# Reordering the forward step of a segment-recurrent attention kernel: K and Q before V, V's second half behind the scores, V rows moved by three engines

## The chip, the cores and the metric

The kernel runs on one core of a Trainium2 chip. A core has engines with a queue of instructions each, which wait for one another through semaphores: TensorE (PE; the loads of its weights are shown apart, as PEld), VectorE (DVE), ScalarE (ACT), GpSimd (POOL) and SyncE (SP), whose queue only issues transfers. PE writes to PSUM, from where DVE and ACT copy ("evict") to SBUF. The metric is the device time of one execution in microseconds, as the median of several runs; lower is better.

## The reference

The program computes a block with a recurrent-memory attention and a SwiGLU feed-forward part, and all gradients. The forward attention is a chain: 2048 tokens are cut into 64 segments of 32, and each segment sees 8 memory rows that the segment before produced.

```python
for s in range(n_seg):                                   # 64
    xs = x[:, s*seg_len:(s+1)*seg_len, :]                # 32 tokens of 448
    h = jnp.concatenate([mem, xs], axis=1)               # 40 rows
    q = jnp.einsum('btd,dhe->bhte', h, Wq)               # 16 heads of 256
    k = jnp.einsum('btd,dhe->bhte', h, Wk)
    v = jnp.einsum('btd,dhe->bhte', h, Wv)
    scores = jnp.einsum('bhqe,bhke->bhqk', q, k) * scale
    scores = jnp.where(mask[None, None], scores, -1000000000.0)
    p = _softmax(scores, axis=-1)
    o = jnp.einsum('bhqk,bhke->bhqe', p, v)
    o = jnp.einsum('bhte,hed->btd', o, Wo)
    mem = o[:, :M, :]                                    # the next segment's memory
    outs.append(o[:, M:, :])
...
h = x + attention(layernorm(x)); out = h + (silu(n @ w_gate) * (n @ w_up)) @ w_down     # n = layernorm(h)
return (out, *gradients of x, mem0, Wq, Wk, Wv, Wo, w_gate, w_up, w_down)
```

## The kernel before

The program has four stages: the forward chain over 64 segments, the feed-forward part with its gradients, the backward chain over the segments, and a tail for weight gradients. The order of instructions on every engine is the order in which the program names them. The change touches only the forward chain, in `forward_chain`, and the helper `spin`.

A segment's 40 rows are treated as two kinds. Of a segment's 32 token columns in `hA`, 8 are the memory (written by the reduction at L518 at the end of the segment before) and 24 are tokens; the last 8 tokens of four segments are gathered in `hB` and projected a tile (four segments) ahead. That work on `hB`, and the Wo product of a tile's `oB` columns, are the "side work": `cur["u1"]`, `cur["u2"]` and `cur["u3"]` are its products (16, 8 and 8 of 512 columns, or 32, 16 and 16 of 224), `cur["e1"]` and `cur["e3"]` its evictions. In the last three segments there is none.

One segment runs thus. The names are those of the code:

- `proj` (L468): one half of K, Q or V, 16 products in four groups of 32 PE columns; the result (128 rows of 512) is evicted to `Kev`, `Qev` or `Vev` by DVE (`V`) or ACT (`A`). In the order: K0, K1, V0, Q0, Q1, and V1 in two pieces.
- `tr_half` (L474): four turnings of 128x128 of `Kev` or `Qev` against the identity; the copies out of PSUM make `kT` and `qT`, whose memory columns POOL fills from the side work (L693, L694).
- `v_shift`: the halves of `Vev` are 32 rows of a group of heads; eight copies of 32x512 put them side by side in `V_sb`, which has one buffer. Six of them are on DVE (`V`, L431), two on POOL (L731). Four row transfers (L646, `v_b_rows`, in SP's queue) add the rows that come from `hB`.
- `scores` (L505) in two halves, into `s_ps`, which holds the mask already (`mask_mm`, L488).
- softmax for each half: maximum (L738), subtraction (L740), exponential on ACT (L742), sum (L745), reciprocal (L747), multiply (L748) into `P_sb`.
- `u1`, `u2`, then `spin` (L847): products of the identity with itself into `s_ps`, which nobody reads before the mask overwrites it; two before the first turning of P (`p_turn`, L761) and one behind it. Then the mask for the next segment, the second turning, `u3`.
- copies of the turned P to `PT` (DVE and ACT), then two `v_shift` copies on DVE, then the product of P and V ("PV", L792) in four groups, evicted to `oA` by DVE and ACT in turns, then the Wo product (L583), the turning of its sum (L513) and the reduction to the next memory (L518).
- stores for the backward part: `KtokA`, `QtokA`, `Vtok` (SP's queue), `P_all` (POOL's queue). In the last segment `ff.load_first` issues six weight loads in POOL's queue.

PSUM has six rotating buffers for all of these (`ps1`) besides the two of the scores.

Of the kernel before, what the change touches and what calls it, by code (L numbers as in the profile page):

```python
# [15 lines left out]
P = 128  # L16
# [390 lines left out]
def forward_chain(k: _K, hA, NWIN, Wq_sb, Wk_sb, Wv_sb, Wo_sb, maskr, work, stage, ff):  # L407
    nc, tc = k.nc, k.tc
    S, D, M, H, Dh, HD = k.S, k.D, k.M, k.H, k.Dh, k.HD
    SEG, L, NSEG, NT, KC, DP, MC, DC = k.SEG, k.L, k.NSEG, k.NT, k.KC, k.DP, k.MC, k.DC  # L410
    X2 = k.aps["A_x"][0]
    ident, identf, dr = k.ident, k.identf, k.dr
# [3 lines left out]
    GF = HD // G  # L416
    NJ = GF // P
    HB = 512
# [6 lines left out]
    def ps1(dtype=FP32):  # L425
        if dtype == FP32:
            return k.pspool.tile([P, 512], FP32, tag="ps", name="psf")
        return k.pspool.tile([P, 1024], BF16, tag="ps", name="psh")

    def V(out, in_):  # L430
        nc.vector.tensor_copy(out=out, in_=in_)  # L431

    def A(out, in_):
        nc.scalar.copy(out=out, in_=in_)

    def slot(s):
        return s % NWIN

# [25 lines left out]
    def proj(ps, W_sb, stat, half, kcs=range(4)):  # L464
        for kc in kcs:
            for g in range(G):
                c0 = g * GF + half * HB
                nc.tensor.matmul(ps[32 * g:32 * g + 32, :], lhsT=stat(kc), rhs=W_sb[0:DB, kc, c0:c0 + HB],  # L468
                                 start=(kc == 0), stop=(kc == KC - 1))

    def tr_half(ev, half):
        pt = ps1(BF16)
        for j in range(4):
            nc.tensor.transpose(pt[:, j * P:(j + 1) * P], ev[:, half * HB + j * P:half * HB + (j + 1) * P], ident[:, :])  # L474
        return pt[:, 0:HB].rearrange("p (j g t) -> p j g t", j=4, g=G)

    def fm_view(dst, half, t0, t1):
        return dst[:].rearrange("p (g j) n -> p j g n", g=G)[:, 4 * half:4 * half + 4, :, t0:t1]
# [4 lines left out]
    S_ps = k.s_ps  # L483
    S_v = [x[0:NR, 0:HQ * L].rearrange("p (h n) -> p h n", n=L) for x in S_ps]

    def mask_mm(half):
        for gg in range(2):
            nc.tensor.matmul(S_ps[half][QB * gg:QB * gg + L, 0:HQ * L], lhsT=ident[0:L, 0:L], rhs=maskr[:, 0:HQ * L],  # L488
                             start=True, stop=False, skip_group_check=True)
# [4 lines left out]
    def hsel(x, half):  # L494
        return x[0:NR].rearrange("p (a b i) n -> p a b i n", a=2, b=2)[:, :, half, :, :]

    def hview(x):
        return x.rearrange("p (a i) n -> p a i n", a=2)
# [87 lines left out]
    def o_units(t):  # L586
        T = tiles[t]
        st = {}

        def mm(i0, i1):  # L590
            for i in range(i0, i1):
                for c in range(4 * i, 4 * i + 4):
                    wo_mm(st["pO"], T.oB[:, c, :], c, c % 2, c < 2, c >= MC - 2)

        def u1():
            st["pO"] = ps1(FP32)
            mm(0, 4)

        def e1():
            pass  # L600

        def u2():
            mm(4, 6)

        def u3():
            mm(6, 8)

        def e3():
            A(partB[:, 0:2 * DB], st["pO"][:, 0:2 * DB])

        def ut():
            st["y"] = turn(partB)

        def et():
            for kc in range(KC):
                gsum(T.aT[0:DB, kc, :].rearrange("p (r j) -> p r j", r=4)[:, :, XA:SEG],
                     st["y"][:, kc, :, :].rearrange("p (r i) g -> p r i g", r=4))
        return dict(u1=u1, e1=e1, u2=u2, u3=u3, e3=e3, ut=ut, et=et)

    def none_units():  # L620
        def f():
            pass
        return dict(u1=f, e1=f, u2=f, u3=f, e3=f, ut=f, et=f)
# [25 lines left out]
    def v_shift(V_sb, Vev, half, gs, eng):  # L649
        for g in gs:  # L650
            gg, g2 = divmod(g, 2)
            o = V_sb[QB * gg:QB * gg + SEG, g2 * GF + half * HB:g2 * GF + (half + 1) * HB]
            eng(o, Vev[32 * g:32 * g + 32, half * HB:(half + 1) * HB])
# [10 lines left out]
    V_sb = work.tile([P, 2 * GF], BF16, name="V_sb", bufs=1)  # L664
# [6 lines left out]
    for s in range(NSEG):  # L671
        t, r = divmod(s, 4)
        sl = slot(s)
        T = tiles[t]
        if r == 0:
# [7 lines left out]
            cur = o_units(t - 1) if t > 0 else none_units()  # L683
        else:
            cur = b_units(t + 1, "?kqv"[r]) if t + 1 < NT else none_units()

        def stat(kc):
            return hA[0:DB, kc, sl, :]

        late2["et"]()  # L690
        kT = work.tile([P, MC, L], BF16, name="kT", bufs=2)
        qT = work.tile([P, MC, L], BF16, name="qT", bufs=2)
# [4 lines left out]
        Kev = work.tile([P, GF], BF16, name="Kev", bufs=1)  # L697
        Qev = work.tile([P, GF], BF16, name="Qev", bufs=1)
        Vev = work.tile([P, GF], BF16, name="Vev", bufs=1)
# [4 lines left out]
        proj(pk1, Wk_sb, stat, 1)  # L704
        A(Kev[:, HB:GF], pk1[:, :])
        nc.sync.dma_start(out=dr["KtokA"][s], in_=Kev[:])
        pv0 = ps1()
        proj(pv0, Wv_sb, stat, 0)
        A(Vev[:, 0:HB], pv0[:, :])
        pq0 = ps1()  # L710
        proj(pq0, Wq_sb, stat, 0)
        V(Qev[:, 0:HB], pq0[:, :])
        A(fm_view(kT, 0, 0, SEG), tr_half(Kev, 0))
        v_shift(V_sb, Vev, 0, (0, 1), V)
        pq1 = ps1()
        proj(pq1, Wq_sb, stat, 1)
        A(Qev[:, HB:GF], pq1[:, :])
        V(fm_view(kT, 1, 0, SEG), tr_half(Kev, 1))
        nc.sync.dma_start(out=dr["QtokA"][s], in_=Qev[:])
        V(fm_view(qT, 0, 0, SEG), tr_half(Qev, 0))  # L720
        v_shift(V_sb, Vev, 0, (2, 3), V)
        if s == NSEG - 1:
            ff.load_first()
        pv1 = ps1()
        proj(pv1, Wv_sb, stat, 1, range(0, 2))
        A(fm_view(qT, 1, 0, SEG), tr_half(Qev, 1))
        proj(pv1, Wv_sb, stat, 1, range(2, 4))
        scores(qT, kT, 0)
        scores(qT, kT, 1)
        A(Vev[:, HB:GF], pv1[:, :])  # L730
        v_shift(V_sb, Vev, 1, (0, 1), lambda out, in_: nc.gpsimd.tensor_copy(out=out, in_=in_))  # L731

        mx, ssum, rs, S_sb = [], [], [], []
        E_sb = work.tile([P, 2, HQ, L], FP32, name="E_sb", bufs=1)
# [1 line left out]
        for half in range(2):  # L736
            mx.append(smal.tile([P, HQ], FP32, name="mx"))
            nc.vector.tensor_reduce(out=mx[half][0:NR], in_=S_v[half], axis=AX.X, op=ALU.max)  # L738
            S_sb.append(work.tile([P, HQ, L], FP32, name="S_sb", bufs=2))
            nc.vector.tensor_tensor(out=S_sb[half][0:NR], in0=S_v[half],  # L740
                                    in1=mx[half][0:NR].unsqueeze(2).to_broadcast([NR, HQ, L]), op=ALU.subtract)
            nc.scalar.activation(out=E_sb[0:NR, half], in_=S_sb[half][0:NR], func=ACT.Exp, scale=k.scale)  # L742
        for half in range(2):
            ssum.append(smal.tile([P, HQ], FP32, name="ssum"))
            nc.vector.tensor_reduce(out=ssum[half][0:NR], in_=E_sb[0:NR, half], axis=AX.X, op=ALU.add)  # L745
            rs.append(smal.tile([P, HQ], FP32, name="rs"))
            nc.vector.reciprocal(out=rs[half][0:NR], in_=ssum[half][0:NR])  # L747
            nc.vector.tensor_tensor(out=hsel(P_sb, half), in0=hview(E_sb[0:NR, half]),  # L748
                                    in1=hview(rs[half][0:NR].unsqueeze(2).to_broadcast([NR, HQ, L])), op=ALU.mult)
        cur["u1"]()  # L750
        cur["e1"]()
        cur["u2"]()
        PT = work.tile([P, HG, L], BF16, name="PT", bufs=2)
        ppt = [ps1(BF16), ps1(BF16)]

        def p_turn(half):
            for gg in range(2):
                b = QB * gg
                for hh in range(HG):
                    if (hh // 2) % 2 == half:  # L760
                        nc.tensor.transpose(ppt[gg][b:b + L, hh * L:(hh + 1) * L], P_sb[b:b + L, hh, :], ident[b:b + L, b:b + L])  # L761
        spin(k, S_ps[0], 2)
        p_turn(0)
        spin(k, S_ps[1], 1)
        if s + 1 < NSEG:
            mask_mm(0)
            mask_mm(1)
        p_turn(1)
        cur["u3"]()
        for gg, eng in ((0, V), (1, A)):  # L770
            b = QB * gg
            eng(PT[b:b + L], ppt[gg][b:b + L, 0:HG * L].rearrange("p (h n) -> p h n", n=L))
        v_shift(V_sb, Vev, 1, (2, 3), V)
        nc.gpsimd.dma_start(out=dr["P_all"][s], in_=P_sb[0:NR].rearrange("p h n -> p (h n)"))

        for gg in range(2):
# [5 lines left out]
        for half in range(2):  # L782
            for gg in range(2):
# [3 lines left out]
                for g in (2 * gg, 2 * gg + 1):  # L787
                    for j in range(4 * half, 4 * half + 4):
# [4 lines left out]
                                         start=True, stop=True)  # L793
# [45 lines left out]
        u[n]()  # L839
    out_pe(NT - 1)  # L840
    out_ev(NT - 1)


def spin(k, ps, n, reps=4):
    x = k.ident[:, :].unsqueeze(1).to_broadcast([P, reps, P])
    for _ in range(n):
        k.nc.tensor.matmul(ps[:, 0:reps * P], lhsT=k.ident[:, :], rhs=x, start=True, stop=True, skip_group_check=True)  # L847


def _get_small(k):  # L850
# [971 lines left out]
```

## Time and profile before

| what | value |
|---|---|
| time, median of 3 runs | 3121.04 us (3116.88 to 3122.59) |
| span of the profiled execution | 3093.7 us |
| what the median has beyond that span | 27.3 us |
| PE busy | 2833.3 us, 92% |
| DVE busy | 1581.8 us, 51% |
| ACT busy | 1091.3 us, 35% |
| POOL busy | 735.9 us, 24% |
| forward chain | about 60 to 1030 us of the span |
| one segment, between two `hA` reductions | 15.05 us |
| `spin` products (L847) | 192 |
| V row copies on DVE, one | 0.285 us |
| V row copies on POOL (L731), one | 0.604 us |

The span is that of one execution under the profiler, from its first instruction to its last; the times of the runs are taken around the whole execution. A busy PE is not the same as a bound PE: an instruction's duration includes its way through the array, products overlap, and a product that nobody needs is busy time too. What sets the end is read from which wait ends last before each step. The granted clock of PE is given as a share of full speed; it is full or half at any moment.

### The profile page before, as it was taken

To read this page: it belongs to the slowest core of one execution; us is meant where nothing else is said; L and a number is where in the kernel's file an instruction comes from. 1 tells how busy PE (TensorE), PEld (TensorE's weight loads), DVE (VectorE), ACT (ScalarE), POOL (GpSimd) and SP (SyncE) were. 2 spreads that over 40 slices of the span, in tenths; PEclk is the share of its full clock that TensorE was granted. 3 is DMA by queue.
4 is the path that set the end of the run, shared out by engine and by line. 5 is a ranking of instruction groups with operands and counts; after the bars stand their busy time and mean duration, and the time that the engine had idled before them with its cause. 6 is when DMAs were issued, how large, how long until landed. Compare 5 with 4: busy or idle time off the path is not lost.

```text
span 3093.7 us, 108443 instructions
## 1 busy us (share of the span) xinstructions
PE 2833.3 (92%) x46568; PEld 1546.5 (50%) x46568; DVE 1581.8 (51%) x4251; ACT 1091.3 (35%) x2831; POOL 735.9 (24%) x1384
## 2 busy tenths in 40 slices
PE   3999999999999699996999999999998899989999
PEld 1555555555555355543555555555555454434454
DVE  4566666566665477763665666565665012212121
ACT  2444444444444356652333333333333011101110
POOL 1222222222222122221222222222222223222332
PEclk9999999999999899997999999999999999989999
DMA  8333333333333863357555565556556899999996
GB/s 260 100 107 118 108 104 106 120 101 107 117 107 97 226 168 117 108 156 164 169 156 136 136 186 147 142 175 154 139 137 208 298 220 200 191 194 203 219 208 134
DMA packets 612448, 482.84 MB, mean 156 GB/s; under 512 B 482944, under 2 KB 526544, under 8 KB 602432
## 3 DMA queue, kind: packets, MB, share of 16 engines
q1 hardware_dynamic: 565632, 289.17, 43.4%
q0 software_dynamic: 46336, 186.74, 17.9%
q8 instruction: 366, 6.00, 0.8%
q14 instruction: 114, 0.93, 0.1%
HBM read 135.08 MB, written 219.52 MB: 115 GB/s over the span
## 4 chain that ended last, share of the span: by engine, by line
PE 70%; DVE 13%; issue 7%; DMA 4%; SPq 3%; ACT 2%; POOL 1%; ACTq 0%; POOLq 0%; DVEq 0%
PE psf L468 15%; PE psf L1668 12%; PE psf L1200 8%; PE psf L583 4%; DVE dO_sb L1164 4%; PE psf L1653 3%; PE psf L1474 3%; PE psf L1173 3%; PE psh L474 3%; PE psf L978 2%; PE psf L1681 2%; PE psf L1061 2%; DMA wall<-in_A_Wv_dram 2%; PE s_ps L847 1%; PE psf L1207 1%
## 5 line engine op out<-in xcount | busy, mean ns | idle before, releaser
L468 PE MATMUL psf<-wall,hA 112*32 112x512 bf16 x6144 | 378.5, 381 | 17.1 <-DVE hA L518 15.3
L1668 PE MATMUL psf<-wall,H_all 128*128 128x512 bf16 x1440 | 323.1, 381 | 14.2 <-DMA wall<-dKA 14.2
L1668 PEld LDWEIGHTS <-H_all 128*128 128x128 bf16 x1440 | 139.4, 98 | 181.7 <-issue 25.2
L468 PEld LDWEIGHTS <-hA 112*32 112x32 bf16 x6144 | 140.1, 96 | 163.3 <-DVE hA L518 31.3
L1580 DVE CAST resc<-psf 128x512 bf16<-128x512 f32 (+1 forms) x58 | 39.0, 673 | 320.9 <-PE psf L1668 286.4
L1164 DVE COPY dO_sb<-dOev 32x512 bf16<-32x512 bf16 x384 | 159.2, 415 | 11.1
L1212 DVE TENSOR_REDUCE dA<-psf 128x32 bf16<-128x128 f32 x63 | 18.4, 292 | 285.7 <-PE psf L1207 285.7
L731 POOL COPY V_sb<-Vev 32x512 bf16<-32x512 bf16 x128 | 77.3, 604 | 340.6 <-PE s_ps L505 330.1
L1524 POOL COPY dmem<-dA 128x32 bf16<-128x32 bf16 x63 | 13.2, 209 | 579.4 <-DVE dA L1212 579.4
L1578 ACT CAST resc<-psf 128x512 bf16<-128x512 f32 (+1 forms) x54 | 31.0, 573 | 333.7 <-PE psf L1668 296.2
L468 PE MATMUL psf<-wall,hB 112*32 112x512 bf16 x1536 | 105.6, 397 | 33.3 <-DMA wall<-in_A_Wk_dram 13.9
L1173 PE MATMUL psf<-wall,dA 128*32 128x512 bf16 x2048 | 123.4, 383 | 13.1 <-DVE dA L1212 13.1
L1200 PE MATMUL psf<-wall,dqA 128*32 128x448 bf16 x2048 | 113.5, 361 | 18.1 <-DMA wall<-in_A_Wq_dram 10.1
L1200 PE MATMUL psf<-wall,dkA 128*32 128x448 bf16 x2048 | 115.8, 371 | 14.2 <-DMA wall<-in_A_Wk_dram 12.6
L1653 PEld LDWEIGHTS <-wall 128*128 128x128 bf16 x864 | 84.4, 99 | 86.4 <-issue 13.1
L583 PE MATMUL psf<-wall,oA 128*32 128x224 bf16 x4096 | 115.1, 267 | 12.0 <-DVE oA L431 11.7
L1200 PE MATMUL psf<-wall,dvA 128*32 128x448 bf16 x2048 | 123.1, 361 | 1.9 <-issue 1.9
L1653 PE MATMUL psf<-dOut_all,wall 128*128 128x448 bf16 x640 | 123.4, 352 | 0.0
L431 DVE COPY V_sb<-Vev 32x512 bf16<-32x512 bf16 x384 | 109.4, 285 | 9.2
L1167 ACT COPY partC<-psf 128x448 f32<-128x448 f32 x64 | 34.0, 532 | 209.6 <-PE psf L1200 209.6
L583 PEld LDWEIGHTS <-oA 128*32 128x32 bf16 x4096 | 97.0, 99 | 20.0 <-DVE oA L431 18.7
L1167 ACT CAST dvA<-psf 128x256 bf16<-128x256 f32 x256 | 85.6, 397 | 59.1 <-PE psf L1474 59.1
(278 smaller groups left out, 5685.2 us busy)
## 6 DMA issues: line engine op xcount, KB each, us to landing
Vtok<-V_sb SPq DMA_DIRECT2D x128, 192.0 KB
KtokA<-Kev SPq DMA_DIRECT2D x64, 256.0 KB
QtokA<-Qev SPq DMA_DIRECT2D x64, 256.0 KB
OTA<-oA POOLq DMA_DIRECT2D x16, 1024.0 KB, 4.5
Q_sb<-QtokA SPq DMA_DIRECT2D x128, 128.0 KB
K_sb<-KtokA SPq DMA_DIRECT2D x128, 128.0 KB
dVA<-dvA POOLq DMA_DIRECT2D x16, 1024.0 KB, 5.2
dKA<-dkA POOLq DMA_DIRECT2D x16, 1024.0 KB, 6.7
```

Of the source, the lines that this page charges most:

```text
L431: nc.vector.tensor_copy(out=out, in_=in_)
L468: nc.tensor.matmul(ps[32 * g:32 * g + 32, :], lhsT=stat(kc), rhs=W_sb[0:DB, kc, c0:c0 + HB], start=(kc == 0), stop=(kc == KC - 1))
L474: nc.tensor.transpose(pt[:, j * P:(j + 1) * P], ev[:, half * HB + j * P:half * HB + (j + 1) * P], ident[:, :])
L583: nc.tensor.matmul(ps[32 * g:32 * g + 32, 0:2 * DB], lhsT=x, rhs=Wo_sb[:, c, a * 2 * DB:(a + 1) * 2 * DB], start=first, stop=last)
L731: v_shift(V_sb, Vev, 1, (0, 1), lambda out, in_: nc.gpsimd.tensor_copy(out=out, in_=in_))
L1164: nc.vector.tensor_copy(out=out, in_=in_)
L1167: nc.scalar.copy(out=out, in_=in_)
L1173: nc.tensor.matmul(ps[32 * g:32 * g + 32, :], lhsT=stat(kc), rhs=WoT_sb[:, kc, c0:c0 + HB], start=(kc == 0), stop=(kc == KC - 1))
L1200: nc.tensor.matmul(pO[32 * g:32 * g + 32, 0:D], lhsT=ch(c), rhs=WT[:, c, :], start=(first and i < 4), stop=(last and i >= MC - 4), skip_gr ...
L1474: nc.tensor.matmul(po[:, n * L:(n + 1) * L], lhsT=lhs[b:b + L, lc:lc + P], rhs=rhs[b:b + L, hh, :], start=True, stop=True)
L1653: nc.tensor.matmul(ps[:, 0:D], lhsT=stat[:, i, c * P:(c + 1) * P], rhs=Y[:, i, 0:D], start=(i == 0), stop=(i == kts - 1))
L1668: nc.tensor.matmul(ps[:, 0:N], lhsT=Hx[:, i, dc * P:(dc + 1) * P], rhs=X[:, i, b * N:(b + 1) * N], start=(i == 0), stop=(i == kts - 1))
```

## The change

K and Q are projected first, then all four turnings, then V's first half; the scores follow; V's second half is projected behind them. `spin` is removed with its three calls. Side work `u2` moves between the mask and the second turning of P. The first half of V is moved to `V_sb` by POOL alone (four copies), the second half by POOL (one), ACT (one) and DVE (two); the evictions of the second half and these copies are named behind the exponentials, and DVE's two copies ahead of the copies to `PT`. Of the four copies to `kT` and `qT`, DVE makes three (before: two). In the last segment the weight loads are named before V's first half.

```diff
+    def G_(out, in_):
+        nc.gpsimd.tensor_copy(out=out, in_=in_)
...
         nc.sync.dma_start(out=dr["KtokA"][s], in_=Kev[:])
+        pq0 = ps1()
+        proj(pq0, Wq_sb, stat, 0)
+        V(Qev[:, 0:HB], pq0[:, :])
+        pq1 = ps1()
+        proj(pq1, Wq_sb, stat, 1)
+        A(Qev[:, HB:GF], pq1[:, :])
+        nc.sync.dma_start(out=dr["QtokA"][s], in_=Qev[:])
+        V(fm_view(kT, 0, 0, SEG), tr_half(Kev, 0))
+        A(fm_view(kT, 1, 0, SEG), tr_half(Kev, 1))
+        V(fm_view(qT, 0, 0, SEG), tr_half(Qev, 0))
+        V(fm_view(qT, 1, 0, SEG), tr_half(Qev, 1))
+        if s == NSEG - 1:
+            ff.load_first()
         pv0 = ps1()
         proj(pv0, Wv_sb, stat, 0)
         A(Vev[:, 0:HB], pv0[:, :])
-        pq0 = ps1()
-        proj(pq0, Wq_sb, stat, 0)
-        V(Qev[:, 0:HB], pq0[:, :])
-        A(fm_view(kT, 0, 0, SEG), tr_half(Kev, 0))
-        v_shift(V_sb, Vev, 0, (0, 1), V)
-        pq1 = ps1()
-        proj(pq1, Wq_sb, stat, 1)
-        A(Qev[:, HB:GF], pq1[:, :])
-        V(fm_view(kT, 1, 0, SEG), tr_half(Kev, 1))
-        nc.sync.dma_start(out=dr["QtokA"][s], in_=Qev[:])
-        V(fm_view(qT, 0, 0, SEG), tr_half(Qev, 0))
-        v_shift(V_sb, Vev, 0, (2, 3), V)
-        if s == NSEG - 1:
-            ff.load_first()
-        pv1 = ps1()
-        proj(pv1, Wv_sb, stat, 1, range(0, 2))
-        A(fm_view(qT, 1, 0, SEG), tr_half(Qev, 1))
-        proj(pv1, Wv_sb, stat, 1, range(2, 4))
+        v_shift(V_sb, Vev, 0, range(4), G_)
         scores(qT, kT, 0)
         scores(qT, kT, 1)
-        A(Vev[:, HB:GF], pv1[:, :])
-        v_shift(V_sb, Vev, 1, (0, 1), lambda out, in_: nc.gpsimd.tensor_copy(out=out, in_=in_))
+        pv1 = ps1()
+        proj(pv1, Wv_sb, stat, 1)
...
             nc.scalar.activation(out=E_sb[0:NR, half], in_=S_sb[half][0:NR], func=ACT.Exp, scale=k.scale)
+        A(Vev[:, HB:GF], pv1[:, :])
+        v_shift(V_sb, Vev, 1, (0,), G_)
+        v_shift(V_sb, Vev, 1, (1,), A)
...
         cur["u1"]()
         cur["e1"]()
-        cur["u2"]()
...
-        spin(k, S_ps[0], 2)
         p_turn(0)
-        spin(k, S_ps[1], 1)
         if s + 1 < NSEG:
             mask_mm(0)
             mask_mm(1)
+        cur["u2"]()
         p_turn(1)
         cur["u3"]()
+        v_shift(V_sb, Vev, 1, (2, 3), V)
         for gg, eng in ((0, V), (1, A)):
             b = QB * gg
             eng(PT[b:b + L], ppt[gg][b:b + L, 0:HG * L].rearrange("p (h n) -> p h n", n=L))
-        v_shift(V_sb, Vev, 1, (2, 3), V)
...
-def spin(k, ps, n, reps=4):
-    x = k.ident[:, :].unsqueeze(1).to_broadcast([P, reps, P])
-    for _ in range(n):
-        k.nc.tensor.matmul(ps[:, 0:reps * P], lhsT=k.ident[:, :], rhs=x, start=True, stop=True, skip_group_check=True)
```

## The prediction, made before the change was run

> **What bounds the kernel now.** I read the page first, for the engines and the granted clock. TensorE (PE) is busy 92% of the span and its clock is near full almost everywhere:
>
> ```profile
> span 3093.7 us, 108443 instructions
> ...
> PEclk9999999999999899997999999999999999989999
> ```
>
> The change lies in the forward step, a loop of 64 segments. In the timeline the reduction that ends a segment (L518, `hA`) returns every 15.05 us from 77 to 980 us (15.29 once; the one segment in four whose side work is the Wo product of the memory rows takes the same); the last three segments, which have no side work, take up to 16.5. So one segment is read closely and multiplied. I take the one from 619.08 to 634.13 and count t from 619.08. The timeline of PE for its second half (start, duration, engine, line, operation):
>
> ```profile
> 626.60 1.48 PE L468 MATMUL psf<-wall,hB 112*32 112x512 bf16 x24
> 628.01 0.61 PE L847 MATMUL s_ps<-ident 128*128 128x512 bf16 x2
> 628.59 0.28 PE L761 MATMUL psh<-ident,P_sb 40*40 40x40 bf16 x8
> 628.81 0.39 PE L847 MATMUL s_ps<-ident 128*128 128x512 bf16 x1
> 629.13 0.32 PE L488 MATMUL s_ps<-maskr,ident 40*40 40x160 bf16 x4
> 629.39 0.28 PE L761 MATMUL psh<-ident,P_sb 40*40 40x40 bf16 x8
> 629.60 0.61 PE L468 MATMUL psf<-wall,hB 112*32 112x512 bf16 x8
> 630.15 0.82 PE L792 MATMUL psf<-PT,V_sb 40*128 40x40 bf16 x32
> 631.16 1.72 PE L583 MATMUL psf<-wall,oA 128*32 128x224 bf16 x64 [0.19 <-DVE oA L431]
> ```
>
> and the timeline of VectorE (DVE) beside it:
>
> ```profile
> 628.21 0.32 DVE L748 TENSOR_TENSOR P_sb<-E_sb,rs 104x160 bf16<-104x160 f32 x1
> 628.46 0.31 DVE L745 TENSOR_REDUCE ssum<-E_sb 104x4 f32<-104x160 f32 x1
> 628.80 0.18 DVE L747 RECIPROCAL rs<-ssum 104x4 f32<-104x4 f32 x1
> 629.01 0.32 DVE L748 TENSOR_TENSOR P_sb<-E_sb,rs 104x160 bf16<-104x160 f32 x1
> 629.70 0.32 DVE L431 COPY PT<-psh 40x320 bf16<-40x320 bf16 x1 [0.36 <-PE psh L761]
> 630.04 0.61 DVE L431 COPY V_sb<-Vev 32x512 bf16<-32x512 bf16 x2
> 630.68 0.42 DVE L431 CAST oA<-psf 128x256 bf16<-128x256 f32 x1
> ```
>
> Two facts. Both turnings of P (L761) start 0.06 us after their multiply (L748) ends, 628.53 and 629.33: PE looks busy, but the softmax chain sets the time and the identity products (L847) fill the wait. And Wo (L583, 631.16) waits for the first `oA` copy, which stands on DVE behind PT and two V row copies.
>
> **The change, part by part.**
>
> *K, Q and turnings first; half of V after the scores.* From t = 3.57 (622.65) to the scores at 6.85 (625.93) PE now has four groups of turnings, one Q and one V projection. Afterwards: turnings at 3.57, 3.80, 4.03 (0.23 apart, as 623.96 to 624.19). The fourth needs Q's second half: its eviction begins at 3.69 (DVE's Qev, 622.77), takes ACT 0.585, and PE follows 0.05 later: 4.33. Then 0.33 for the turning and 0.98 for the V projection (622.98 to 623.96): scores at 5.64, which is 1.21 earlier. K, Q and kT, qT copies end by 5.3 and hide in this. The whole softmax chain moves by 1.21 if DVE and ACT are free, and they are: ACT's V half goes at 5.76 to 6.34, the first exponential at 6.95.
>
> *Filling.* After the scores (0.67) PE has 16 products of V and 16 of the side work, 0.435 per eight (24 take 1.41): free at 8.16. Without the L847 products, 192 in all, it then waits for the turning. Removing them frees no time where softmax sets the end; their price is in the clock, below.
>
> *V rows.* DVE had six copies, POOL two. Now POOL has five, ACT one, DVE two. POOL starts 0.06 after the V half (626.64, 626.70), and copies follow every 0.66: 6.40, 7.06, 7.73, 8.39, then the fifth. PE reads them first at 10.6, so the copies themselves are covered; without that cover 3.3 us would stand on the path. ACT's copy (no such row; between 0.2 and 0.6 us by its `oB` and Vev rows) fits between 8.3 and the side eviction. What is not covered is what POOL does to DVE. In the backward part the same two copies run side by side:
>
> ```profile
> 1396.58 1.27 POOL L1435 COPY dO_sb<-dOev 32x512 bf16<-32x512 bf16 x2 [0.69 <-ACT dOev L1167]
> 1396.66 1.96 DVE L1164 COPY dO_sb<-dOev 32x512 bf16<-32x512 bf16 x4
> ```
>
> DVE's L1164 copies take 282 ns alone and up to 700 beside L1435: a copy started during one of POOL's ends 0.15 us after it. POOL's stay at 607 (worst 757). In this forward loop POOL and DVE copies never met; now they do, and so does L748.
>
> L748 beside a POOL copy is shown nowhere. Bounds: nothing (L745, which reads the same `E_sb`, takes 310 beside L731 and away from it), or the wait of L1164. I take the wait: L748, like L1164, writes a whole tile in SBUF from SBUF, while L745 writes four numbers a row. So: first multiply due at 9.13 - 1.21 = 7.92, inside POOL's third copy (7.73 to 8.33): ends 8.52 (0.15 after it, 0.04 for its greater length). Turning 0 at 8.57. Second multiply 0.48 later, 9.00 to 9.32. PE: turning 0.21, mask at most 0.26 (say 0.19), side work 0.55: turning 1 at 9.52, after P is ready at 9.38.
>
> The Trainium skill, "SBUF — State Buffer", "Who interferes with whom", says that a VectorE instruction with both inputs in SBUF contends with GpSimd's reads, and copies in the two-port modes do too, while reductions do not. The L1164 and L745 rows agree; no run here shows the multiply. By it the multiply waits, and the sum is the one made here.
>
> Then DVE: POOL's fifth copy begins about 9.05, shares with the multiply and ends near 9.75; DVE's first V copy waits until 9.90, the second ends 10.21, PT is copied 10.24 to 10.56, PE starts PV at 10.62 (now 11.07). Its own order would have allowed 10.28. With no V copies behind PT, `oA` follows at once: first group of eight products 0.35 to DVE's start (sixteen take 0.53, ACT's `oA` at 630.68), 0.42 copy, 0.06 to PE: Wo at 11.46 against 12.08. **Gain 0.62 us a segment**; the rest of the segment is unchanged, so 64 x 0.62 = 39.7 us.
>
> *Queues.* In SP's queue Q's store goes earlier and Vtok's first store waits for POOL's fifth copy (about 9.8 instead of 8.9); a store lands 2.8 after its issue (630.68 to 633.52, where the row transfer that waits for it starts), and the four row transfers behind it end about 0.7 into the next segment, as now. PV needs them ten us later. POOL's P_all issue (0.55) waits behind the fifth copy, nobody waits for it within two segments. In the last segment POOL's six weight loads (3.7 us from 1014.8) end before its first copy. Nothing is added for these.
>
> *Clock.* In segment 61, without side work, the clock was halved. The busy time by stretches (us, PE, PEld, DVE, ACT, POOL busy, clock):
>
> ```profile
> 987.90:991.30 3.40, 1.71 (x25) 0.79 (x25) 2.80 (x12) 1.02 (x3) 1.67 (x3) 1.00 0.25 58
> 991.30:994.70 3.40, 3.26 (x84) 2.79 (x87) 1.54 (x6) 1.05 (x5) 0.08 (x1) 0.50 0.36 87
> ```
>
> A thin stretch, then one of about 3.4 us at 0.50. The segment took 16.19, so a drop costs 1.14 us. Weighing each product by the share of the 128x128 array that it uses, the thin stretch held 0.71 us of whole-array time (three identity products are 0.64). The thinnest stretch of a usual segment, from 627.7, held 1.23 and was kept. Afterwards the thinnest, from 8.0 to 11.4, holds 16 side products (0.75), PV (0.17) and turnings and mask (0.06): 0.97. That is between. Weighed so over the whole run, a drop followed on stretches up to 1.08 and on only two above that (1.28), and stretches were kept from 1.09 on. A stretch under 1.09 needs its start within some 0.3 us, of 3.4: one segment in eleven, so 5 or 6 drops of 64, say 5 x 1.14 = 5.7 us.
>
> The Trainium skill, "TensorE: Matmul & The Clock Gate", "HAM oscillation", gives as abstract rule that PE must not idle over about 3.4 us. By it no drop comes, and the sum would be 5.7 us lower. The stretch at 987.9, where PE's longest pause is 0.80 us (before 989.79), speaks against it, and the measurement decides.
>
> **Sum.** 39.7 - 5.7 = 34.0 us off the span of 3093.7: 3059.7. The median of three runs, 3121.04, is 27.3 above the span (start and end around it), which stays: **3087 us**.
>
> **The rivals.**
>
> *The multiplies do not wait* (L745's row holds). Turning 0 at 8.32; the second multiply ends 9.04, DVE's V copies 10.11, PV 10.52, Wo 11.35: 0.73 a segment, 46.7, with three drops 3.4: 3121 - 43 = 3078. Both rows speak equally of SBUF sources; the two-source form speaks against.
>
> *No collision at all* (211 of 384 L1164 copies took 282 ns). Then V copies end 9.66, PT 10.01, PV 10.07, Wo 10.90: 1.18 a segment, 75.5, thinnest stretch above 1.3, no drops: 3046. Against: POOL's copies fill 6.4 to 9.7 without a gap that DVE could use.
>
> *The clock, on the other side.* If the identity products were what held the clock, each segment's thin stretch halves it: 64 x (1.14 - 0.62) = +33, 3154. It is slower from 35 drops on. For it: 0.97 lies nearer the dropped 0.71 than the kept 1.23 does. Against: slices seem to run freely, and only those that start in the right tenth see so little.
>
> *POOL becomes the bound.* At its worst row, 757 ns, five copies end at 10.5, V copies at 11.0, Wo at 12.19: 0.11 later than now, +7, with drops 3134. Against: 757 was seen once in 128.
>
> *It does not do what it says*: excluded; in the built order PE has 192 products fewer, and of the 512 V row copies DVE does 128 instead of 384, POOL 320 instead of 128, ACT 64.
>
> **How the numbers follow.** Forecast 45%, multiplies free 20%, no collision 7%, clock 8%, POOL 5%; 15% for gains partly lost to a wait that I don't see, spread over 3095 to 3130. From no change 0.2% can just be told, 3114.8 and 3127.3. Faster: 45 + 20 + 7 and half of the 15: 0.79. Same 0.07, slower 0.14. The range leaves out half of the no-collision case, clock, POOL and part of the unseen: 3058 to 3114. The forecast's own: 3080 to 3097 (1 to 14 drops).
>
> **What would show it.** Period 14.4 us between `hA` reductions; scores 1.2 earlier; L748 and V copies on DVE at 0.45 to 0.75 us beside POOL's; PV at 10.6, Wo at 11.5; a few slices of clock 0.50 between 80 and 980 us. It is wrong if L748 stays at 324 ns (then 14.3), if the clock falls in most segments, or if PV waits on POOL's rows.

## The result, and the profile after

The changed kernel takes 3123.54 us (median of 20 runs, 3110.21 to 3143.18), the kernel before 3118.72 us in 20 runs beside it. The ratio on record is 1.0041, with a 95% interval of 1.0021 to 1.0060: slower, by 6.5 to 18.7 us. (It is not the quotient of the two medians, which lie 4.8 us apart; the ratios below are those on record too.) The forecast was 3087 us and faster.

The page of the changed kernel, span and granted clock of PE in 40 equal parts of 78 us:

```profile
span 3129.9 us, 108267 instructions
...
PEclk8999999999999899997999999999998999898999
```

The digits hardly differ from those of before, and the mean clock only falls from 0.977 to 0.955. The loss sits below the resolution of this line. It shows where one looks at each segment's end. VectorE's timeline, cut to the reductions into `hA` (start, duration, engine, line, operation, and in brackets how long DVE had been idle and on what it waited):

```profile
592.20 0.23 DVE L521 TENSOR_REDUCE hA<-psf 112x32 bf16<-112x64 f32 x1 [2.04 <-PE psf L516]
...
608.32 0.23 DVE L521 TENSOR_REDUCE hA<-psf 112x32 bf16<-112x64 f32 x1 [3.51 <-PE psf L516]
...
622.97 0.23 DVE L521 TENSOR_REDUCE hA<-psf 112x32 bf16<-112x64 f32 x1 [1.96 <-PE psf L516]
...
639.18 0.22 DVE L521 TENSOR_REDUCE hA<-psf 112x32 bf16<-112x64 f32 x1 [3.50 <-PE psf L516]
...
653.87 0.22 DVE L521 TENSOR_REDUCE hA<-psf 112x32 bf16<-112x64 f32 x1 [2.05 <-PE psf L516]
```

Segments of about 14.65 and 16.15 us alternate (16.12, 14.65, 16.21, 14.69). In the long ones DVE waits 1.5 us more for PE at the end. The busy time by stretches shows why (us, then PE, PEld, DVE, ACT and POOL busy with instructions in brackets, PE's granted clock, share and GB/s of the transfers):

```profile
631.50:634.80 3.30, 2.40 (x64) 1.32 (x65) 2.52 (x8) 1.55 (x4) 2.13 (x4) 1.00 0.29 51
634.90:638.20 3.30, 3.30 (x74) 2.52 (x68) 0.77 (x4) 0.85 (x4) 0.00 (x0) 0.50 0.32 95
```

A stretch of about 3.4 us in which PE waits twice (for the first turning of P, then for PV) and in between runs products that fill only a part of the array is followed by one at half clock. Here that one holds the Wo product:

```profile
635.08 3.18 PE L586 MATMUL psf<-wall,oA 128*32 128x224 bf16 x64
```

It takes 3.18 us there and 1.72 where the clock is full. From here on such a length of 3.4 us is called a slice of the clock, a segment with a slice at half clock is called halved, and the others undisturbed. The stretches at half clock begin at 573.40, 604.12, 634.84, 665.56 and 696.28: every 30.72 us, and one is 3.413 us long, so they are exactly nine of their own length apart. A pair of segments (14.65 + 16.12 = 30.77, less where a segment is 14.56) also takes nine such lengths. The loop has fallen in step with the clock's slices, and every second segment is caught.

Over the 59 segments between the first 60 reductions, before had none halved and a mean of 15.054 us. After has 27 halved ones of 16.12 us, 31 of 14.644 us and one of 15.23 us. So 59 x (15.054 - 14.644) = 24.2 us were won, 27 x (16.12 - 14.644) = 39.9 us lost, and the sum, 15.7 us more, with 0.6 of the one at 15.23, is what the chain shows (59 x (15.331 - 15.054) = 16.3 us).

The undisturbed segment is close to the forecast. PE from 616 us on, in the segment whose first product starts at 608.60 (t counts from there; it is one of those whose side work is the Wo product of `oB`, while the prediction read one with projections of `hB`):

```profile
617.30 0.22 PE L762 MATMUL psh<-ident,P_sb 40*40 40x40 bf16 x3 [0.58 <-DVE P_sb L750]
...
618.15 0.28 PE L762 MATMUL psh<-ident,P_sb 40*40 40x40 bf16 x8
...
619.37 1.03 PE L792 MATMUL psf<-PT,V_sb 40*128 40x40 bf16 x32 [0.45 <-DVE PT L431]
620.34 1.72 PE L586 MATMUL psf<-wall,oA 128*32 128x224 bf16 x64
```

And VectorE and POOL beside it:

```profile
616.52 0.73 DVE L750 TENSOR_TENSOR P_sb<-E_sb,rs 104x160 bf16<-104x160 f32 x1
...
617.73 0.33 DVE L750 TENSOR_TENSOR P_sb<-E_sb,rs 104x160 bf16<-104x160 f32 x1
618.09 0.89 DVE L431 COPY V_sb<-Vev 32x512 bf16<-32x512 bf16 x2
619.01 0.32 DVE L431 COPY PT<-psh 40x320 bf16<-40x320 bf16 x1
...
615.14 3.38 POOL L437 COPY V_sb<-Vev 32x512 bf16<-32x512 bf16 x5 [3.50 <-ACT Vev L434]
```

L750 is the multiply that was L748. The first one takes 0.73 us instead of 0.32, and two V copies 0.89 instead of about 0.6; POOL's five copies run beside both, from 615.14 to 618.52. The two waits of PE in brackets, 0.58 and 0.45 us, lie in the part of the segment on which the slice before a half clock falls. The groups by form over the whole run say the same (count, busy us, mean ns of one, idle before):

```profile
L437 POOL COPY V_sb<-Vev 32x512 bf16<-32x512 bf16 x320 | 201.5, 630 | 284.2 <-ACT Vev L434 269.3
L750 DVE TENSOR_TENSOR P_sb<-E_sb,rs 104x160 bf16<-104x160 f32 x128 | 67.1, 525 | 4.6 <-DVE rs L749 0.3
L431 DVE COPY V_sb<-Vev 32x512 bf16<-32x512 bf16 x128 | 55.6, 434 | 3.0
L434 ACT COPY V_sb<-Vev 32x512 bf16<-32x512 bf16 x64 | 39.5, 617 | 2.1
```

525 is about the mean of 729 and 325, 434 about that of 587 and 287: each segment's first multiply and first V copy wait, the second ones don't.

### The profile page after: what moved, and what is told of

It is laid out like the page before. It is cut to its first block, busy times and chain, and to the rows that moved or that the text cites. A ratio compares the mean times of both kernels' runs of the same rounds, so it can differ in the third digit from the quotient of the medians.

```text
span 3129.9 us, 108267 instructions
## 1 busy us (share of the span) xinstructions
PE 2810.7 (90%) x46340; PEld 1572.9 (50%) x46376; DVE 1587.3 (51%) x4059; ACT 1082.4 (35%) x2831; POOL 863.9 (28%) x1576
## 4 chain that ended last, share of the span: by engine, by line
PE 63%; DVE 16%; issue 7%; DMA 6%; SPq 4%; ACT 3%; POOL 1%; ACTq 0%; POOLq 0%; DVEq 0%
PE psf L1662 11%; PE psf L471 10%; PE psf L1194 8%; PE psf L586 5%; DVE dO_sb L1158 4%; PE psf L1647 3%; PE psf L972 3%; PE psf L1468 3%; PE psf L1167 2%; PE psh L477 2%; PE psf L1055 2%; PE psf L1675 2%; PE psf L792 2%; DVE V_sb L431 2%; DMA wall<-in_A_Wv_dram 1%
## 5 line engine op out<-in xcount | busy, mean ns | idle before, releaser
L471 PE MATMUL psf<-wall,hA 112*32 112x512 bf16 x6144 | 368.7, 381 | 17.2 <-DVE hA L521 15.2
L437 POOL COPY V_sb<-Vev 32x512 bf16<-32x512 bf16 x320 | 201.5, 630 | 284.2 <-ACT Vev L434 269.3
L471 PEld LDWEIGHTS <-hA 112*32 112x32 bf16 x6144 | 146.5, 96 | 167.7 <-DVE hA L521 31.1
L586 PE MATMUL psf<-wall,oA 128*32 128x224 bf16 x4096 | 153.5, 322 | 0.4
L471 PE MATMUL psf<-wall,hB 112*32 112x512 bf16 x1536 | 113.4, 397 | 26.9 <-DMA wall<-in_A_Wv_dram 9.5
L586 PEld LDWEIGHTS <-oA 128*32 128x32 bf16 x4096 | 122.5, 119 | 15.8
L1194 PE MATMUL pob<-wall 128*32 128x448 bf16 x1536 | 105.8, 356 | 0.0
L1161 ACT CAST wall<-psf 128x64 bf16<-128x64 f32 x512 | 105.6, 243 | 0.0
```

The source lines that it names most:

```text
L586: nc.tensor.matmul(ps[32 * g:32 * g + 32, 0:2 * DB], lhsT=x, rhs=Wo_sb[:, c, a * 2 * DB:(a + 1) * 2 * DB], start=first, stop=last)
L1194: nc.tensor.matmul(pO[32 * g:32 * g + 32, 0:D], lhsT=ch(c), rhs=WT[:, c, :], start=(first and i < 4), stop=(last and i >= MC - 4), skip_gr ...
```

## The experiments

Two questions: is it the clock, and by what part of the change; and do POOL's copies hold up the multiply? In all runs the times are compared with those of the kernel before on the same chip. The table further down gives, for each, what the trace shows of the chain.

**The identity products back in the changed kernel (e1).**

```diff
+        spin(k, S_ps[0], 2)
         p_turn(0)
+        spin(k, S_ps[1], 1)
```

> The changed kernel with the three identity products put back (two ahead of the first turning of P, one behind it), everything else as changed. Theory 1 (the clock): in the changed kernel two segments alternate, 14.6 us and 16.1 us, and the second has a slice of 3.4 us at half clock; the identity products put 0.64 us of whole-array time back into the thin stretch, so no slice between 80 and 980 us is at 0.50, every segment takes 14.6 to 14.7 us, and the forward chain (63 hA reductions) is 61 x 0.7 = about 43 us shorter than in the changed kernel and 25 us shorter than in the kernel before: ratio to before about 0.992. Rival (the reordered step itself, or the V rows on POOL, cost the time): the period stays near 15.35 on average and the ratio near 1.004.

Measured: 3087.17 us, ratio 0.9887 (0.9850 to 0.9924). No segment between the first 60 reductions is halved, and the reductions come every 14.67 us:

```profile
602.66 0.23 DVE L521 TENSOR_REDUCE hA<-psf 112x32 bf16<-112x64 f32 x1 [2.00 <-PE psf L516]
...
617.33 0.23 DVE L521 TENSOR_REDUCE hA<-psf 112x32 bf16<-112x64 f32 x1 [2.05 <-PE psf L516]
```

So three products that nobody reads turn the change from a loss into a gain of 1.1%. The undisturbed period did not grow (14.665 against 14.644): they lie in PE's waits.

**The identity products out of the kernel before, and nothing else (e2).**

```diff
-        spin(k, S_ps[0], 2)
         p_turn(0)
-        spin(k, S_ps[1], 1)
```

> The kernel before with the three identity products left out and nothing else changed. Theory 1 (the clock): its thin stretch, from the end of the side work to Wo, then holds about 0.83 us of whole-array time in 3.4 us, under the 1.15 up to which slices of the changed kernel were followed by half clock; a third to a half of the segments are slowed by 1.1 to 1.5 us, mean period 15.5 to 15.8, forward chain 30 to 45 us longer than before, ratio 1.01 to 1.015. Rival (the products are only filling): clock full, period 15.05, ratio 1.000.

Measured: 3157.97 us, ratio 1.0114 (1.0076 to 1.0151), with 33 of 59 segments halved and an undisturbed period of 15.049 us, which is that of before. Its reductions:

```profile
567.10 0.23 DVE L518 TENSOR_REDUCE hA<-psf 112x32 bf16<-112x64 f32 x1 [2.15 <-PE psf L513]
...
583.59 0.23 DVE L518 TENSOR_REDUCE hA<-psf 112x32 bf16<-112x64 f32 x1 [3.59 <-PE psf L513]
...
599.98 0.23 DVE L518 TENSOR_REDUCE hA<-psf 112x32 bf16<-112x64 f32 x1 [3.50 <-PE psf L513]
...
615.03 0.23 DVE L518 TENSOR_REDUCE hA<-psf 112x32 bf16<-112x64 f32 x1 [2.15 <-PE psf L513]
```

Two long segments (16.49, 16.39), one short (15.05): 47.93 us, near 14 slices (47.79). That is a little more than theory 1 had: 56% of the segments and a mean of 15.85 us, against a third to a half and 15.5 to 15.8. Removing the products alone costs 1.1%; with e1, the missing products are the reason why the change is slower.

**POOL kept away from the multiply (e3).** This kernel leaves out three of POOL's five V row copies (the second half of V's first half, and group 0 of its second half), so those rows of `V_sb` are not written; no identity products.

```diff
-        v_shift(V_sb, Vev, 0, range(4), G_)
+        v_shift(V_sb, Vev, 0, (0, 1), G_)
...
-        v_shift(V_sb, Vev, 1, (0,), G_)
```

> The changed kernel (no identity products) with three of POOL's five V row copies left out, two of the first half and the one of the second half (these rows of V are not brought in, so the product of P and V works on stale rows). It shows what POOL's copies cost DVE, and whether the clock falls for want of the identity products or for the waiting. Theory (port): the multiplies at L748 take 324 ns again instead of 729, DVE's two V copies 0.28 each, P and V start near t = 10.1 and Wo near 11.0; undisturbed period 13.9 to 14.0. The thin stretch then holds about 1.3 us, over the 1.21 that was kept, so no slice is at half clock (few, if any). Rival A (no port): L748 stays at 0.7 or the period stays at 14.6. Rival B (the identity products are needed as such): half-clock slices return every second or third segment although the wait is gone.

Measured: 3049.4 us in one run, period 13.94 us. VectorE in the same place as above:

```profile
569.88 0.32 DVE L749 TENSOR_TENSOR P_sb<-E_sb,rs 104x160 bf16<-104x160 f32 x1
...
571.04 0.59 DVE L431 COPY V_sb<-Vev 32x512 bf16<-32x512 bf16 x2
```

The multiply takes 0.32 us again, and both V copies 0.59 together. With POOL's copies gone from beside them both waits are gone, worth 0.7 us a segment here. And only 1 of 59 segments is halved without any identity product: filling PE's waits and removing the waits have the same effect on the clock.

**ACT makes the copy that met DVE's V copies (e4), identity products as before.**

```diff
-        v_shift(V_sb, Vev, 1, (0,), G_)
-        v_shift(V_sb, Vev, 1, (1,), A)
+        v_shift(V_sb, Vev, 1, (0, 1), A)
```

> The first experiment with POOL's fifth copy (second half, first group) moved to ACT as a second copy there. Theory (port): DVE's two V copies, no longer beside a POOL copy, take 0.28 each; PT is copied about 0.3 us earlier and the period is 14.3, no half-clock slices; ratio to before about 0.985. ACT does it between 9.0 and 9.6, ahead of the side eviction. Rival (ACT becomes the bound, since its copy of PT is pushed back behind the side eviction): period 14.6 or more.

Measured: 3070.51 us, ratio 0.9851 (0.9820 to 0.9881). DVE's V copies fall to 0.284 and 0.290 us, as expected, but the period is 14.58 and not 14.3: a miss. P was ready for the second turning at 9.49 us after the reduction, and the turning began at 10.07. The third identity product, then the mask and `u2`, stood before it on PE. Before the change this product had covered a wait; here the wait was shorter than what stood before the turning, as the next run confirms.

**The same without the third product (e5).**

```diff
         spin(k, S_ps[0], 2)
         p_turn(0)
-        spin(k, S_ps[1], 1)
```

> The changed kernel with ACT instead of POOL copying V group 0 of the second half, and two identity products before the first turning of P (the run before this one, e4, had a third behind it). In e4 the third product put the mask 0.32 us later on PE, and the mask and u2 put the second turning at 10.07 us while its P was ready at 9.49. Theory 1 (the softmax and PE order set the end; the clock falls where a slice of 3.41 us holds under about 1.1 us of whole-array time): the second turning at 9.75, PV at 10.52, period of an undisturbed segment 14.27 (e4 14.59); the thinnest slice holds 1.35 - 0.21 = 1.14 or a little more, at the edge, so under 10 halved segments; median ratio to before 0.978 to 0.984. Rival (turning 1 is late for another reason than the third product): period 14.5 to 14.6 and ratio 0.985 as in e4. Rival (any product less than three lets the clock fall): every second or third segment halved, ratio 0.988 or more.

Measured: 3065.91 us, ratio 0.9851 (0.9823 to 0.9879); period 14.34, no segment halved. The second turning starts 9.64 us after the reduction, 0.43 earlier than in e4, and PV 10.61 (in the one segment in four with Wo as its side work 9.59 and 10.52). VectorE in one of the latter (the reduction before it ends at 574.21):

```profile
582.18 0.72 DVE L749 TENSOR_TENSOR P_sb<-E_sb,rs 104x160 bf16<-104x160 f32 x1
...
583.38 0.33 DVE L749 TENSOR_TENSOR P_sb<-E_sb,rs 104x160 bf16<-104x160 f32 x1
583.73 0.59 DVE L431 COPY V_sb<-Vev 32x512 bf16<-32x512 bf16 x2
584.35 0.32 DVE L431 COPY PT<-psh 40x320 bf16<-40x320 bf16 x1
```

The period fell as theory 1 had it, 14.27 expected. The ratio missed: 0.978 to 0.984 was expected, and 0.9851 is the rival's, that of e4. Yet e4 is the one that does not fit its chain. From the first to the last reduction of the profiles, e5 is 45 us shorter than before, and its ratio means 46 us; e4 is 31 us shorter, and its ratio means 46 (37 to 56). What the rest of e4's gain is stays open; the two were timed on different occasions. Together with e4 this is the fastest version, 1.5% under the kernel before; its first multiply still waits 0.4 us for POOL.

**The same without any (e6).**

```diff
-        spin(k, S_ps[0], 2)
         p_turn(0)
```

> The changed kernel with ACT instead of POOL copying V group 0 of the second half and no identity products. Undisturbed period as in e5, since the products lie in the wait for the first turning: 14.27 us. Theory 1 (thin slices of under about 1.1 us are followed by half clock, and the loop falls in step with the slices): halved segments return, one in three (3 x 14.27 + 1.45 = 44.26, 13 slices of 3.413 are 44.37) or one in two, mean period 14.7 to 15.0, ratio 0.990 to 1.000. Rival (the clock in the changed kernel fell because of the longer wait behind the POOL copies, and the identity products are not needed once that wait is shorter, as in e3 where almost no segment was halved without them): under 6 halved segments, ratio 0.977 to 0.981.

Measured: 3077.4 us, ratio 0.9889 (0.9853 to 0.9926); undisturbed period 14.35 as in e5, 10 of 59 halved, irregularly (the slices at half clock lie 30.7, 44.4, 116 or 174 us apart). Halved segments return, as theory 1 had it, but fewer than it gave: mean period 14.61, not 14.7 to 15.0, and a ratio between the two theories, just under the 0.990 of theory 1.

**The changed kernel with one product (e7).**

```diff
+        spin(k, S_ps[0], 1)
         p_turn(0)
```

> The changed kernel with a single identity product of 512 columns (0.21 us of whole-array time) before the first turning of P. Undisturbed period 14.62 to 14.67 in every theory. Theory 1 (the whole-array time in the thinnest slice decides, with an edge between 1.1 and 1.2 us): slices that held 0.95 to 1.15 hold 1.16 to 1.36, so halved segments fall from about 29 to under 10; ratio 0.988 to 0.993. Rival (the clock needs the wait to be filled, whatever the amount: one product leaves most of it open): about as many halved segments as in the changed kernel, 20 to 30, ratio 0.999 to 1.004.

Measured: 3118.2 us, ratio 1.0025 (0.9997 to 1.0054), 25 of 59 halved at an undisturbed 14.64. This went to the rival: one product is almost as bad as none. Its reductions alternate like those of the changed kernel:

```profile
584.92 0.23 DVE L521 TENSOR_REDUCE hA<-psf 112x32 bf16<-112x64 f32 x1 [2.05 <-PE psf L516]
...
601.05 0.23 DVE L521 TENSOR_REDUCE hA<-psf 112x32 bf16<-112x64 f32 x1 [3.50 <-PE psf L516]
...
615.72 0.23 DVE L521 TENSOR_REDUCE hA<-psf 112x32 bf16<-112x64 f32 x1 [1.96 <-PE psf L516]
```

**What the runs say together.** For each profiled execution I took its undisturbed segments, let a stretch of 3.413 us begin at every 0.02 us of one, and summed the whole-array time of the products that start in it, as the prediction weighs them (each by the share of the array that it uses). The table gives how long, in the median segment, the starts are whose stretch holds under 1.09 us (the prediction's edge) and under 1.25 us (the fullest stretch followed by half clock in the forward loop of e2, e6 and e7).

| kernel | identity products a segment | undisturbed segment, us | starts under 1.09 / under 1.25, us | halved of 59 | mean segment, us |
|---|---|---|---|---|---|
| before | 3 | 15.05 | 0 / 0.09 | 0 | 15.05 |
| after | 0 | 14.64 | 0.84 / 1.24 | 27 | 15.33 |
| e1 | 3 | 14.67 | 0 / 0.01 | 0 | 14.67 |
| e2 | 0 | 15.05 | 1.02 / 1.53 | 33 | 15.85 |
| e3 | 0 | 13.94 | 0 / 0.17 | 1 | 13.97 |
| e4 | 3 | 14.58 | 0 / 0 | 0 | 14.59 |
| e5 | 2 | 14.34 | 0 / 0 | 0 | 14.35 |
| e6 | 0 | 14.35 | 0.32 / 0.80 | 10 | 14.61 |
| e7 | 1 | 14.64 | 0.31 / 0.88 | 25 | 15.26 |

The length of the thin starts sorts the kernels, whether identity products or shorter waits made it small. Slices that began at random would catch the share length / 3.413: for after 0.84 to 1.24, so 15 to 21 of 59, for e2 18 to 26, for e6 6 to 14, for e7 5 to 15. e6 lies inside that; after, e2 and e7 lie above. After and e7 have a pair of segments that takes nine slices (14.65 + 16.12), while e6's mean pair, 14.35 + 15.89 = 30.24, is 0.48 us short of it; where its halved segments were longer (16.42 and 16.14 us) it too was caught twice at 30.7 us, and then lost step. e6 and e7 differ in the row that ACT copies too, and no run changed the period alone, so that being in step explains the excess is argued, with the 30.72 us of the trace behind it. An estimate from the table speaks for it: lay slices of 3.413 us end to end over 59 segments of each kernel's undisturbed length, let a segment be halved, and so longer, whenever a slice begins in its thin starts, and average over where the first slice lies. With nothing random in it, this gives 26 (edge 1.09) to 30 (edge 1.25) halved segments for after, 24 to 41 for e2, 0 to 4 for e3, 5 to 22 for e6 and 16 to 27 for e7; measured were 27, 33, 1, 10 and 25. The edge is not sharp: some stretches of 1.09 to 1.13 us in e2, e6 and e7, and one of 0.97 in e7, were kept. Some products may be missing from a trace, and the weighing may not be what the clock goes by.

## Why the prediction was wrong

*The step that failed* is in the part on the clock: "A stretch under 1.09 needs its start within some 0.3 us, of 3.4: one segment in eleven, so 5 or 6 drops of 64, say 5 x 1.14 = 5.7 us." The mechanism was right, and the thinness nearly: it gave 0.97 us for the thinnest stretch, and the 27 slices of after that were followed by half clock hold 0.87 to 1.15. Three sizes were wrong. The starts that see less than 1.09 us last 0.84 us, not 0.3 (1.24 us with the edge at 1.25): the prediction sums only the thinnest position, not every start, and its edge came from one run. At random, 0.84 us would already have caught 16 of 64 segments. The slices do not seem to meet the segments at random either: a pair of segments, one of them halved, comes to nine slices. And one halved segment costs 1.48 us, not the 1.14 of segment 61: the slice lies on the whole Wo product, which takes 3.18 us instead of 1.72. In segment 61 it took 2.85, and there was no side work; the segment after it, 16.52 us long with a Wo of 3.18, had already shown the larger price. In place of 5.7 us the term was 27 x 1.48 = 39.9 us. Even the full 0.62 us a segment, 36.6 us over 59, would not have paid for that.

The "thinnest stretch of a usual segment, from 627.7", which "held 1.23 and was kept", was no test of the edge. Counted from the half-clock slice at 991.32, the slices of before begin there at 626.09 and 629.51 and hold 1.94 and 2.08 us.

The rival on the other side, in which every segment's thin stretch halves the clock, was the one that happened, in about half of the segments; it had been given 8%. Its turning point of 35 halved segments lies at 16 with the measured sizes (24.2 / 1.48). The reason against it, "only those that start in the right tenth see so little", is the same failed step.

The Trainium skill, "TensorE: Matmul & The Clock Gate", "HAM oscillation", names idle gaps of more than about 3.4 us as the danger. In the slice from 631.5 PE's waits are 0.48 and 0.44 us and half clock follows, so here the measurement is far stricter than that rule, as the prediction had it from one slice of before.

*The gain of 0.62 us a segment* was 0.41 (15.054 - 14.644). By its steps, in t: scores 5.64, measured 614.24 - 608.60 = 5.64. First multiply at 7.92 and waiting: 7.92, and 0.73 us long. POOL's third copy, behind which it waits, ended 0.14 later than said, because the V half's eviction began at 5.89 and not 5.76; the turning at 8.70 instead of 8.57. Second turning 9.55 (9.52). PT 10.41 (10.24) and PV 10.77 (10.62): POOL's fifth copy met the second multiply as forecast, but took 0.72 us, and DVE's first V copy beside it ended at 10.07 instead of 9.90. PV to Wo 0.97 (0.84): the rest of the miss, Wo at 11.74 (11.46). In an undisturbed segment with `hB` as its side work (from 577.80) the second turning starts at 9.59, PV at 10.87 and Wo at 11.76. e3 shows that POOL's copies cause the waits, so the main line was right against "no collision", whose period, 15.05 - 1.18 = 13.87 us, is nearly what e3 shows once those copies are gone. "The multiplies do not wait" fell: each segment's first takes 729 ns.

The Trainium skill, "SBUF — State Buffer", "Who interferes with whom", has it that a VectorE instruction with two inputs in SBUF contends with GpSimd's reads. No run of before could show it; after and e3 do, 729 ns beside POOL's copy and 325 without.

*"27.3 above the span (start and end around it)"* failed too. The run whose span is 3129.9 us took 3131.76: 1.9 us lie around a span. Before's profiled execution was a quick one. From the last reduction into `hA` to the end, where no kernel here differs, the nine profiled executions take 2080.8 (before) to 2107.5 us (e3), most of the difference behind the backward chain (717 to 747 us from POOL's last copy into `dO_sb`). Since the code there is the same, a comparison of single spans seems to carry some 25 us that are not the change's; the times of the chain don't. One profile of each kernel can't show more.

*Queues and ACT's row* gave no surprise: the copy on ACT takes 617 ns, just above the 0.2 to 0.6 us that were given, and PV's wait ends with DVE's copy to `PT` (its bracket above), not with a transfer.

## What to carry to other kernels

Before removing work that looks useless, ask which waits of TensorE it fills: in a loop whose matmuls are thin, sum the whole-array time in every stretch as long as the clock's slice, for every start and not for one, and multiply the share of thin starts by what half clock costs where the dense product stands. Do not count on chance to spread such hits, since a periodic loop can fall in step with the slices. Then shorten the waits rather than fill them where that can be done: taking a copy off POOL that a VectorE instruction had to wait for helped both the path and the clock.

## What the runs showed of the hardware

- The half-clock slices of the forward loop are 3.413 us long and lie at whole multiples of that length: 30.72 us = 9 of them, from 573.40 to 696.28 us in after, and in e6, where the halved segments come irregularly, 9, 13, 34 and 51 of them (30.72, 44.38, 116.05 and 174.08 us). So the loop adjusts to them, not they to the loop.
- In the forward loop half clock followed slices in which PE had work most of the time (in after 2.40 of 3.30 us busy by the profile, no wait over 0.58 us). Slices with 1.27 us of whole-array time or more were always kept there.
- An identity product of 512 columns, 0.21 us of array time as weighed here (the two of a pair start 0.23 us apart in before), does little by itself: one a segment leaves 25 of 59 segments halved (e7), three leave none (e1). Two are enough where the waits are shorter (e5), none is needed for all but one segment where they are gone (e3).
- VectorE's multiply of a 104x160 tile took 325 ns alone and 729 beside POOL's copy; a copy of 32x512 took 284 to 290 ns and 587. The waiting instruction ended 0.15 to 0.17 us after POOL's. POOL's own copy, begun beside the second multiply, took 718 ns instead of 606. ACT made the same copy in 617 ns, and DVE did not wait for it: in e5 the second multiply took 0.33 us beside two of ACT's.
